# Transposing a layer norm by DMA out of DRAM in place of TensorE, from the fifth token tile on

## The chip, the core and the metric

The kernel runs on one core of a Trainium2 chip. A core has engines that run in parallel, each working through its own instructions in a fixed order: PE (matrix multiply, and transposes as a kind of matmul), DVE (vector work), ACT (activation functions, here mostly exponentials and some copies), POOL (small vector work) and SP, which in this kernel only issues DMA transfers. SBUF is the on-chip memory with 128 partitions, PSUM is where PE writes its results, and DRAM lies outside the core. An engine that reaches an instruction whose input isn't there waits, and everything behind it on that engine waits too. The metric is the device time of one execution in microseconds (us); less is better.

## What is computed

Two kinds of blocks are applied in turn, twice: attention with 32 heads of size 20, and a two-layer perceptron that mixes over the tokens. S is 2048 tokens, D is 640 features, F is 1536. All inputs are bf16.

```python
def _A_ref(x, wqkv, wo):                       # attention block
    qkv = (x @ wqkv).reshape(B, S, 3, H, Dh)   # (then transposed to 3, B, H, S, Dh)
    scores = jnp.einsum("bhqd,bhkd->bhqk", q, k) * (Dh ** -0.5)
    p = _softmax(scores, axis=-1)
    o = jnp.einsum("bhqk,bhkd->bhqd", p, v)
    return o.transpose(0, 2, 1, 3).reshape(B, S, D) @ wo

def _B_ref(x, w1, b1, w2, b2):                 # token-mixing perceptron
    h = _layernorm(x, axis=-1)
    u = _gelu(jnp.einsum("bsd,sf->bdf", h, w1) + b1)
    y = jnp.einsum("bdf,fs->bds", u, w2) + b2
    return y.transpose(0, 2, 1)

x = x + _A_ref(_layernorm(x), wqkv, wo)
x = x + _B_ref(_layernorm(x), w1, b1, w2, b2)
# ... and the same two lines once more
```

"Layer 0" and "layer 1" below are the first and the second pair of these lines.

## The kernel before

**Tiles.** The 2048 tokens are 16 token tiles of 128. For Q, K and V the layer norm of x is needed with the features on the partitions, so each normalized token tile (128 tokens x 640 features) is transposed in five squares of 128 x 128 into the buffer `hT`, which lies in the region `hh` and is 5 x 2048 columns wide. Attention works in units of a query block of 512 tokens, a group of four heads (there are eight groups) and a key tile of 128 tokens; each unit has four chunks, one for each head. A chunk is a score matmul (line 700, on PE), an exponential, and a value matmul (line 927). The exponential of most chunks is one ACT instruction (line 887, two or three chunks each); for the rest DVE builds it from one step on each chunk (line 840) and five on each unit (line 860).

**How a token tile gets to be transposed.** `token_tile` (line 521) makes the statistics on DVE (lines 343 to 346), the reciprocal root on POOL (354 and 356), applies both on DVE (line 530) into one of three bf16 buffers `hbf`, held by the ring `rHB`, and calls `transposes` (line 537). That one queues five PE transposes against an identity (line 541) into a PSUM bank and one copy of 128 x 640 from there into `hT` on ACT or DVE (line 547; in the profile the helper's lines 461 and 463). The buffer goes back to the ring when PE has read it. `got_hT` then releases the V projection of this tile, and, when four tiles are there, the K projections of these four for the first four groups (and for the first four tiles Q too). So a K projection waits for four tiles at a time; K1, K2 and K3 are those of tiles 4 to 7, 8 to 11 and 12 to 15.

**Where the tiles come from.** In layer 0 they are loaded from the input at the start (`front`, line 1556, `load_x0`), into eight buffers that come free when the tile has been applied. In layer 1 each is the result of the perceptron's second matmul in layer 0 (`add_mm2`, line 1327), which runs tile by tile while layer 1's attention has already begun on the first four tiles. Each such tile is also stored (`x2d`).

**What sets the order.** The program plans itself when it is built: every engine has a queue of jobs with a due rank and a planned duration, `run_until` picks the job that can begin first by the planner's clock, and the order so found is fixed in the program. Work that fills PE between the units of attention, such as projections and transposes, goes through `add_fill`; during attention two PSUM banks (5 and 7) serve these fills and the scores for DVE. All DMAs of `dma` (line 270) are issued by SP in one order; the planner takes 420 ns for an issue, and at most eight are open at a time. A DMA with `needs` is planned only after another one is planned to have landed. On the chip the order stays as planned, whatever the true durations are.

Of the kernel before, what the change touches and what calls it, by code (L numbers as in the profile page):

```python
# [11 lines left out]
BF16 = mybir.dt.bfloat16  # L12
# [8 lines left out]
D = 640  # L21
H = 32
DH = 20
NG = 8
NDT = D // 128
# [29 lines left out]
FILL_FIRST = False  # L55
MM1_U = ((280, 384), (408, 470))
VLATE = 1.0
PAD_V = 450.0
N_WARM0 = 10
STEPS0 = ((0, 4), (4, 16))  # L60
# [8 lines left out]
LAT_V = 120.0  # L69
EXP_CH = 453.0  # L70
D_SLACK = 0.0
WIN_S = (160.0, 160.0)
FILL_OVER = 0.0
M_F = 0.0
SD_WAIT = 500.0
# [7 lines left out]
DMA_RATE = 400.0  # L83
# [43 lines left out]
def kernel(  # L127
# [12 lines left out]
    nc = tc.nc  # L140
    S = A_x.shape[1]
    F = B_w1.shape[1]
    assert A_x.shape[2] == D
    NT = S // 128
    NKT = NT
# [11 lines left out]
    dpool = ctx.enter_context(tc.tile_pool(name="dpool", bufs=1, space=DRAM))  # L157
    mem = ctx.enter_context(tc.tile_pool(name="mem", bufs=1))
    psp = ctx.enter_context(tc.tile_pool(name="psp", bufs=1, space=PSUM))
    x1d = [dpool.tile([S, D], F32, name=f"x1d{i}") for i in range(2)]  # L160
    x2d = dpool.tile([S, D], F32, name="x2d")
    uacca = [dpool.tile([F, D], F32, name=f"uacca{i}") for i in range(2)]
    uacc = [dpool.tile([F, D], F32, name=f"uacc{i}") for i in range(2)]

# [102 lines left out]
    landed = {}  # L267
    dma_last = deque(maxlen=8)

    def dma(out_, in_, nbytes, ready=0.0, then=None, rate=DMA_RATE, key=None, needs=None, prio=1):  # L270

        def when():
            return max([ready] + ([dma_last[0]] if len(dma_last) == 8 else []) + ([landed[needs]] if needs else []))

        def f(start):
            nc.sync.dma_start(out=out_, in_=in_)
            dma_clk[0] = max(dma_clk[0], start + DMA_LAT) + nbytes / rate
            land = dma_clk[0] + 600.0
            dma_last.append(land)
            if key is not None:  # L280
                landed[key] = land
            if then:
                then(land)
        push("SP", prio, when, 420.0, f, ok=(lambda: needs in landed) if needs else None)
# [230 lines left out]
    def make_producer(L):  # L515
        def load_wv():
            L.wv = sb("wv", [128, NDT, D], BF16)
            dma(L.wv[:], A_wqkv[:, 2 * D:3 * D].rearrange("(dt p) n -> p dt n", p=128), 128 * NDT * D * 2,
                then=lambda t: setattr(L, "wv_ready", t))

        def token_tile(tt, src, ready, release=None):

            def got_stats(mv, r):
                scale_job(0, r, mv, lambda rt, nmr, r2: apply_(mv, rt, r2), False)

            def apply_(mv, rt, r):
                def f(start):
                    sl = rHB.take()
                    h_bf = sb("hbf", [128, D], BF16, sl)
                    nc.vector.tensor_scalar(out=h_bf[:], in0=src, scalar1=mv[:, 0:1], scalar2=rt[:, 0:1],  # L530
                                            op0=ALU.subtract, op1=ALU.mult)
                    if release:
                        release(start + 450)
                    transposes(h_bf, sl, start + 450 + LAT_V)
                push("DVE", 1 if tt < 4 else 2, r, 450, f, ok=lambda: len(rHB) > 0)

            def transposes(h_bf, sl, r):
                mms = []
                for dt_ in range(NDT):
                    def mm(t, dt_=dt_):  # L540
                        pe(nc.tensor.transpose(t[:, dt_, :], h_bf[:, dt_ * 128:(dt_ + 1) * 128], ident[:]))
                    mms.append(mm)

                def evac(eng, t, s, e):
                    if L.hT is None:
                        L.hT = sb("hh", [128, NDT, S], BF16)
                    copy(eng, L.hT[:, :, tt * 128:(tt + 1) * 128], t[:])
                    got_hT(tt, e)
                add_fill(mms, 64.0, evac, 420.0, ready=r, pr=L.need[("T", tt // 4)] - 0.5, urgent=lambda: L.urgent(("T", tt // 4)), acost=720.0, eprio=0.5, bf16=[128, NDT, 128],
                         after=lambda t: rHB.give(sl, t + LAT_PE))  # L550
            prio = 1 if tt < 4 else 2
            stats_job(prio, ready, src, got_stats)

        def got_hT(tt, ready):
            tb = tt // 4
            L.h_left[tb] -= 1
            if L.h_left[tb] == 0:
                for g in range(L.nearly):
                    if tb == 0:
                        add_proj("Q", g, 0, ready)  # L560
                    add_proj("K", g, tb, ready)
            add_v(tt, ready)

        def add_v(tt, ready):
            for half, (c0, c1) in enumerate(COLS):
                key = ("V", tt, half)

                lo, hi = L.last_step, NKT * L.nearly
                pr = L.need[key] + 0.5 if half == 0 else lo + (hi - lo) * VLATE * (tt + 1) / NT
                mms = []  # L570
                for dt_ in range(NDT):
                    def mm(t, dt_=dt_, c0=c0, c1=c1):
                        mmul(t[:, 0:c1 - c0], lhsT=L.hT[:, dt_, tt * 128:(tt + 1) * 128],
                                            rhs=L.wv[:, dt_, c0:c1], start=(dt_ == 0), stop=(dt_ == NDT - 1))
                    mms.append(mm)

                def evac(eng, t, s, e, c0=c0, c1=c1, half=half):
                    copy(eng, Vv[:, tt, c0 // DH:c1 // DH, 0:DH], t[:, 0:c1 - c0].rearrange("p (h i) -> p h i", i=DH))
                    L.v_ready[(tt, half)] = e
                    L.v_left[half] -= 1  # L580
                    if half == 0 and L.v_left[0] == 0:
                        producer_done()
                add_fill(mms, 136.0, evac, 400.0, ready=lambda: max(ready, L.wv_ready), pr=pr,
                         urgent=lambda pr=pr: pr <= L.now_unit() + URG, acost=460.0, ok=lambda: L.wv_ready is not None)

        def add_proj(what, g, b, ready):
            w = wk_pad if what == "K" else wq_pad
            tb = b
            key = (what, g, b)
            mms = []  # L590
            for dt_ in range(NDT):
                def mm(t, dt_=dt_):
                    mmul(t[:, :], lhsT=w[:, dt_, g, :], rhs=L.hT[:, dt_, tb * 512:(tb + 1) * 512],
                                        start=(dt_ == 0), stop=(dt_ == NDT - 1))
                mms.append(mm)
            box = {}

            def on_start(s):
                if what == "Q":
                    box["slot"] = rQ.take()  # L600

            def evac(eng, t, s, e):
                if what == "Q":
                    L.qslot[(b, g)] = box["slot"]
                    L.QT[(b, g)] = sb("QT", [128, 512], BF16, box["slot"])
                    dst = L.QT[(b, g)][:]
                else:
                    if g not in L.KT:
                        L.KT[g] = sb("KT", [128, S], BF16, g)
                    dst = L.KT[g][:, tb * 512:(tb + 1) * 512]  # L610
                copy(eng, dst, t[:, :])
                L.qk_ready[key] = e
                L.kq_left -= 1
                if L.all_kq and L.kq_left == 0:
                    L.on_hT_dead()
            L.kq_left += 1
            pr = L.need[key]
            if what == "Q" and b == LASTQB:

                pr = min(pr, L.need[("Q", 0, b)] + g)  # L620
            add_fill(mms, PE_MM, evac, 600.0, ready=ready, pr=pr, ok=lambda: w_left[what] == 0 and (what == "K" or len(rQ) > 0),
                     urgent=lambda: pr <= L.now_unit() + URG, acost=620.0, on_start=on_start, what=what)

        def producer_done():
            L.prod_done = True
            for g in range(L.nearly, NG):
                for tb in range(NQB):
                    add_proj("K", g, tb, 0.0)
                add_proj("Q", g, 0, 0.0)
            for qb in range(1, NQB):  # L630
                for g in range(NG):
                    add_proj("Q", g, qb, 0.0)
            L.all_kq = True

        L.load_wv, L.token_tile = load_wv, token_tile

    def make_attention(L):
# [4 lines left out]
        a_ptr = [0]  # L642
# [459 lines left out]
        L.opt_J, L.do_J, L.opt_T, L.do_T, L.d_take, L.opt_exp, L.do_exp = opt_J, do_J, opt_T, do_T, d_take, opt_exp, do_exp  # L1102
        L.urgent = urgent
        L.next_slot = lambda: nS[0] % 2
        L.now_unit = lambda: a_ptr[0]
        L.x1last = {}

# [293 lines left out]
    def pe_choose():  # L1401
# [5 lines left out]
        opts = []  # L1407
        s_at[0] = 1e18
        if a is not None and not a.done:
            sa = a.opt_SA()  # L1410
            if sa is not None:
                s_at[0] = st_(sa, "row")
                opts.append((s_at[0], 0, WIN_S[a.next_slot()], a.do_SA))
            sd = a.opt_SD()
            if sd is not None:
                opts.append((st_(sd, "row"), 0.9, 120, a.do_SD))
# [240 lines left out]
```

## Time and profile before

| | |
|---|---|
| runs | 1769.47, 1761.27 and 1764.65 us; median 1764.65 |
| profiled execution | 1763.39 us; span of the trace 1761.6 us; mean PE clock 0.992 |
| PE transposes (line 541) | 160, of 219 ns each |
| copies of transposed tiles | 19 on ACT (692 ns), 13 on DVE (480 ns) |
| DMA | 98.10 MB, 17.6% of the 16 DMA engines' time on SP's queue |

A line of the profile has the engine, the line of the kernel, the operation, output <- inputs, the shape and the number of instructions. In a timeline the first two numbers are start and length in us, several equal instructions may be merged (x12), and the bracket at the end gives the idle time before it and the instruction that ended it. A group that names several numbers in ns gives least, median and greatest. Matmuls overlap, so that busy time of PE is not the time at its peak.

### The profile page before, as it was taken

The page shows a single profiled execution, that of the slowest core. Times are in us where ns is not written, and L with a number is a line of the kernel's source. Part 1 is how long each engine was busy: PE and PEld are TensorE (multiplying, and loading weights), DVE is VectorE, ACT ScalarE, POOL GpSimd, SP SyncE. Part 2 cuts the span into 40 slices and gives each one's busy share as a digit, 9 for nine tenths or more (in the row PEclk, how much of TensorE's full clock was granted, in tenths as well). Part 3 has the DMA queues.
Part 4 walks back from the last instruction along what each step waited for, and adds up shares of the span by engine and source line. Part 5 has one row for each costly group of instructions (what it writes and reads, how often), then busy time and mean ns, then how long its engine had stood idle before and what let it go on. Part 6 is the DMA issues. An engine that isn't in the chain of part 4 may idle for free.

```text
span 1761.6 us, 50941 instructions
## 1 busy us (share of the span) xinstructions
PE 1673.1 (95%) x22105; PEld 644.4 (37%) x22105; DVE 1531.1 (87%) x2715; ACT 1589.0 (90%) x1441; POOL 181.1 (10%) x297
## 2 busy tenths in 40 slices
PE   8999999999999999998999999999999999999989
PEld 3433233222333233334545432332333333333356
DVE  6788999999989999998444699999998999989973
ACT  7799999999999999997598799999999999999940
POOL 3100012000200020002100000210012000200010
PEclk8999999999999999999999999999999999999999
DMA  3200001000222015520422000100012210365133
GB/s 117 28 2 2 2 13 35 1 2 1 62 71 63 17 40 183 164 62 21 141 71 81 32 2 2 39 24 1 1 31 70 69 59 1 122 181 174 46 96 97
DMA packets 103298, 98.10 MB, mean 56 GB/s; under 512 B 45600, under 2 KB 79520, under 8 KB 103072
## 3 DMA queue, kind: packets, MB, share of 16 engines
q1 hardware_dynamic: 99456, 94.82, 17.6%
q8 instruction: 173, 2.83, 0.7%
q0 software_dynamic: 3616, 0.01, 0.3%
q14 instruction: 53, 0.43, 0.1%
HBM read 63.35 MB, written 31.46 MB: 54 GB/s over the span
## 4 chain that ended last, share of the span: by engine, by line
PE 45%; DVE 41%; ACT 7%; issue 4%; DMA 2%; POOL 1%; SPq 0%; DVEq 0%; POOLq 0%; ACTq 0%
DVE JT L860 17%; PE pst L456 15%; DVE JT L840 14%; PE pst L700 12%; PE pst L927 12%; ACT P L887 6%; PE pst L453 5%; DVE T_85 L976 2%; DVE attnT L1003 1%; DMA W<-in_B_w_dram 1%; DVE QT L463 1%; DVE x1last L1088 1%; DVE bnst L343 1%; DVE bnst L344 1%; DVE rden L988 1%
## 5 line engine op out<-in xcount | busy, mean ns | idle before, releaser
L887 ACT ACTIVATE P<-pst 128x1024 bf16<-128x1024 f32 (+1 forms) x1321 | 1512.5, 1273 | 42.8 <-PE pst L700 26.3
L860 DVE TENSOR_SCALAR JT<-JT 128x2048 uint16<-128x2048 uint16 x995 | 669.7, 703 | 3.2
L700 PE MATMUL pst<-QT,KT 32*128 32x512 bf16 (+1 forms) x4224 | 577.0, 377 | 33.9 <-ACT P L887 20.7
L840 DVE TENSOR_SCALAR JT<-pst 128x512 uint16<-128x512 f32 x796 | 528.0, 677 | 66.9 <-PE pst L700 47.7
L927 PE MATMUL pst<-P,Vaug 128*32 128x512 bf16 (+1 forms) x3396 | 516.3, 380 | 3.1 <-DVE T_85 L976 2.2
L927 PE MATMUL pst<-JT,Vaug 128*32 128x512 bf16 (+1 forms) x4140 | 499.9, 376 | 14.7 <-DVE T_85 L976 9.1
L700 PEld LDWEIGHTS <-KT 32*128 32x128 bf16 x4224 | 155.1, 91 | 501.4 <-issue 492.5
L927 PEld LDWEIGHTS <-Vaug 128*32 128x32 bf16 x7536 | 181.9, 94 | 319.3 <-issue 284.8
L995 POOL TENSOR_TENSOR T_86<-T_85,rden 128x512 bf16<-128x512 f32 x64 | 68.2, 1065 | 1184.4 <-DVE rden L988 1144.7
L1466 PE MATMUL pst<-ident,zw 128*32 128x512 bf16 (+1 forms) x390 | 125.7, 376 | 0.0
L456 PEld LDWEIGHTS <-W 128*32 128x32 bf16 x3384 | 88.7, 96 | 63.3 <-issue 31.5
L456 PE MATMUL pst<-wo,attnT 128*32 128x320 bf16 x1984 | 105.2, 301 | 3.7 <-DVE JT L840 1.4
L456 PE MATMUL pst<-hh,wq 128*32 128x512 bf16 x1232 | 102.9, 382 | 2.3 <-DVE JT L840 1.8
L456 PE MATMUL pst<-hh,wk 128*32 128x512 bf16 x1240 | 96.9, 381 | 1.5 <-DVE hh L463 0.7
L456 PE MATMUL pst<-x1last,W 128*32 128x320 bf16 x1536 | 81.6, 301 | 0.4
L456 PEld LDWEIGHTS <-attnT 128*32 128x32 bf16 x1984 | 49.6, 95 | 48.4 <-issue 32.4
L456 PE MATMUL pst<-attnT,hh 128*32 128x320 bf16 x1196 | 58.9, 300 | 3.2 <-ACT hh L461 0.7
L456 PE MATMUL pst<-JT,W 128*32 128x320 bf16 x1080 | 52.6, 300 | 0.3 <-issue 0.3
L1003 DVE STREAM_TRANSPOSE attnT<-T_86 128x512 bf16<-128x512 bf16 (+1 forms) x66 | 44.9, 682 | 2.1 <-POOL T_86 L995 2.0
L1466 PEld LDWEIGHTS <-zw 128*32 128x32 bf16 x390 | 35.2, 96 | 31.1 <-issue 17.3
L456 PE MATMUL pst<-hh,W 128*32 128x320 bf16 x768 | 40.5, 301 | 6.0 <-DMA W<-in_B_w_dram 4.7
L456 PEld LDWEIGHTS <-wq 128*32 128x32 bf16 x1232 | 32.6, 95 | 34.4 <-issue 20.2
(94 smaller groups left out, 893.4 us busy)
## 6 DMA issues: line engine op xcount, KB each, us to landing
W<-in_B_w_dram SPq DMA_DIRECT2D x10, 768.0 KB
W<-in_B_w_dram SPq DMA_DIRECT2D x24, 256.0 KB
xs<-in_A_x_dram SPq DMA_DIRECT2D x32, 160.0 KB
x2d<-xs SPq DMA_DIRECT2D x16, 320.0 KB
xs<-x2d SPq DMA_DIRECT2D x16, 320.0 KB
x1d_69<-xs SPq DMA_DIRECT2D x12, 320.0 KB
uacca_72<-W SPq DMA_DIRECT2D x12, 320.0 KB
W<-uacca_72 SPq DMA_DIRECT2D x12, 320.0 KB
```

Source lines behind the costliest of these rows:

```text
L343: nc.vector.bn_stats(out=bst[:, 0, :], in_=src[:, 0:half])
L453: nc.tensor.matmul(out_, lhsT=lhsT, rhs=rhs, start=start, stop=stop)
L456: nc.tensor.matmul(out_[32 * c:32 * c + 32], lhsT=lhsT[:, 32 * c:32 * c + 32], rhs=rhs, start=start, stop=stop, tile_position=(0, 32 * c))
L700: pe(nc.tensor.matmul(dst, lhsT=k_, rhs=q_, start=True, stop=True, tile_position=(32 * j, 0)))
L840: nc.vector.tensor_scalar(out=c["jt"][:, j * 512:(j + 1) * 512], in0=Dt[:], scalar1=SCALE * LOG2E * 256.0, scalar2=127.0 * 256.0, op0=ALU. ...
L860: nc.vector.tensor_scalar(out=tt_[:], in0=c["jt"][:], scalar1=0.5, scalar2=TERM_C[i], op0=ALU.mult, op1=ALU.add)
L887: nc.scalar.activation(out=P[:, 0:n, :].rearrange("p a b -> p (a b)"), in_=St[:, 0:n, :].rearrange("p a b -> p (a b)"), func=ACT.Exp, scal ...
L927: pe(nc.tensor.matmul(dst, lhsT=Vaug[:, n:n + 32], rhs=ap, start=acc["cnt"][j] == 1 and not part, stop=last[j] and (half is None or part = ...
L976: nc.vector.transpose(out=T1[:], in_=src[:, 0:w])
L995: eng.tensor_tensor(out=T2[:], in0=T1v, in1=rden.unsqueeze(2).to_broadcast([128, w // 32, 32]), op=ALU.mult)
L1003: nc.vector.transpose(out=attnT[(qb, g)][:, q0:q1], in_=T2[:].rearrange("p c i -> p (c i)"))
L1466: pe(nc.tensor.matmul(dst[0:32, 0:128 * n], lhsT=zw[:, 0:32], rhs=ident[:].unsqueeze(1).to_broadcast([128, n, 128]), start=not inside, sto ...
```

## The change

For token tiles 4 to 15, in both layers, the normalized tile isn't transposed on PE. It is stored to a DRAM buffer `hd` (160 KB a tile), and after every second tile five transposing DMAs read 256 tokens x 128 features each out of `hd` and write 128 x 256 into `hT`. The store gives the `hbf` buffer back when it has landed; `got_hT` is called for both tiles when the fifth transposing DMA is planned to have landed. All of these DMAs are issued on SP, with rank 0.5, ahead of ordinary transfers (rank 1). The planner gives a transposing DMA the same 420 ns of issue and half the ordinary rate. The other edits give the score window a value for each stage (all equal to the old ones) and add a condition to the rank of the second half of V.

```diff
+T_DMA = 4
-WIN_S = (160.0, 160.0)
+WIN_S = ((160.0, 160.0), (160.0, 160.0), (160.0, 160.0))
...
+    hd = [dpool.tile([S, D], BF16, name=f"hd{i}") for i in range(2)]
...
         def f(start):
-            nc.sync.dma_start(out=out_, in_=in_)
+            if transpose:
+                nc.sync.dma_start_transpose(out_, in_)
+            else:
+                nc.sync.dma_start(out=out_, in_=in_)
...
             def transposes(h_bf, sl, r):
+                if tt >= T_DMA:
+
+                    dma(hd[L.layer][tt * 128:(tt + 1) * 128, :], h_bf[:], 128 * D * 2, r, then=lambda t: rHB.give(sl, t), key=("h", L.layer, tt),
+                        prio=0.5)
+                    if tt % 2:
+                        if L.hT is None:
+                            L.hT = sb("hh", [128, NDT, S], BF16)
+                        for dt_ in range(NDT):
+                            def got(t, dt_=dt_):
+                                if dt_ == NDT - 1:
+                                    got_hT(tt - 1, t)
+                                    got_hT(tt, t)
+                            dma(L.hT[:, dt_, (tt - 1) * 128:(tt + 1) * 128], hd[L.layer][(tt - 1) * 128:(tt + 1) * 128, dt_ * 128:(dt_ + 1) * 128],
+                                256 * 256, needs=("h", L.layer, tt), then=got, rate=DMA_RATE * 0.5, transpose=True, prio=0.5)
+                    return
...
-                pr = L.need[key] + 0.5 if half == 0 else lo + (hi - lo) * VLATE * (tt + 1) / NT
+                pr = L.need[key] + 0.5 if half == 0 or L.nearly > NG // 2 else lo + (hi - lo) * VLATE * (tt + 1) / NT
...
+        L.stage = lambda: 0 if not L.prod_done else 1 if a_ptr[0] < NG * NKT else 2
...
-                opts.append((s_at[0], 0, WIN_S[a.next_slot()], a.do_SA))
+                opts.append((s_at[0], 0, WIN_S[a.stage()][a.next_slot()], a.do_SA))
```

More of the change, by code (lines that the diff above doesn't have):

```diff
@@ L268, with dma @@
     dma_last = deque(maxlen=8)
-    def dma(out_, in_, nbytes, ready=0.0, then=None, rate=DMA_RATE, key=None, needs=None, prio=1):
+    def dma(out_, in_, nbytes, ready=0.0, then=None, rate=DMA_RATE, key=None, needs=None, prio=1, transpose=False):
         def when():
```

## The prediction, made before the changed kernel had run

> **What bounds the kernel now.** I read the page first, then the stretches by window, the timelines of PE, ACT, DVE and SP in the two places where the layer norm is transposed, and last the built order of both kernels, which shows what stands behind what on each in-order engine.
>
> ```profile
> PE 1673.1 (95%) x22105; PEld 644.4 (37%) x22105; DVE 1531.1 (87%) x2715; ACT 1589.0 (90%) x1441; POOL 181.1 (10%) x297
> ```
> Over the span these three engines share the limit. By window (length, then busy PE, PEld, DVE, ACT, POOL, then clock and DMA):
>
> ```profile
> 30.00:42.00 12.00, 11.36 (x136) 4.32 (x138) 9.39 (x21) 11.98 (x11) 2.05 (x6) 1.00 0.06 15
> 42.00:54.00 12.00, 10.44 (x169) 4.85 (x166) 8.92 (x16) 7.54 (x10) 6.79 (x3) 1.00 0.65 43
> 935.00:978.00 43.00, 41.26 (x773) 21.50 (x768) 15.88 (x32) 35.08 (x39) 3.36 (x9) 1.00 0.21 70
> ```
> At 42 to 54 no engine is full: this stage waits on a chain. At 935 to 978, the last layer-0 tiles, PE is the limit (96%).
>
> ```profile
> 43.38 3.71 ACT L887 ACTIVATE P<-pst 128x1536 bf16<-128x1536 f32 x3 [0.21 <-PE pst L700]
> 52.30 0.45 PE L541 MATMUL pst<-ident,attnT 128*128 128x128 bf16 x5
> 53.75 0.62 PE L456 MATMUL pst<-hh,wk 128*32 128x512 bf16 x8 [0.66 <-DVE hh L463]
> 55.10 13.68 ACT L887 ACTIVATE P<-pst 128x1024 bf16<-128x1024 f32 x12 [2.26 <-PE pst L927]
> 72.81 1.25 PE L456 MATMUL pst<-hh,wk 128*32 128x512 bf16 x20
> ```
> In layer 0 the exponentials stop at 47.1 and resume at 55.1 because the keys of tiles 8 to 11 wait for their transposes; those of tiles 12 to 15 are made at 72.8 (K3). I take K3 as the mark of this stage.
>
> ```profile
> 44.56 0.68 DVE L463 CAST KT<-pst 128x512 bf16<-128x512 f32 x1
> 22.32 1.11 DVE L530 TENSOR_SCALAR attnT<-xs,mv,rt 128x640 bf16<-128x640 bf16 x3
> L276 SPq DMA_DIRECT2D x2d<-xs x16: 319/423/862, 843.5 to 972.1; - x16
> L461 ACT COPY hh<-pst x19: 692/692/699, 10.3 to 975.2; 128x640 bf16<-128x640 bf16 x19
> L463 DVE COPY hh<-pst x13: 435/480/492, 12.1 to 895.1; 128x640 bf16<-128x640 bf16 x13
> ```
> The first line copies out the keys of tiles 4 to 7 for group 0 (K1), ready at 45.2; an ordinary DMA issue holds SP 0.42 us.
>
> [...] The trace has 219 ns on PE, five overlapped in 0.45 us; no run yet shows the DMA. [...] the first transpose of a group waits for the stores' semaphores. [...]
>
> **The change, part by part.**
> *Removed:* 12 tiles in each of 2 layers: 120 PE transposes, 24 x 0.45 = 10.8 us of PE, and 24 copies; the built order has 22 fewer on ACT (15.2 us) and 2 fewer on DVE. Neither is all on the path: in layer 0 the stage waits on the chain; in layer 1 PE is the limit: 12 x 0.45 = 5.4 us, with 1.6 us of short PE idles around these transposes, together 7.
>
> *Two edits of no effect:* the windows by stage hold the same 160, and the V priority needs more than four early groups, which there are not.
>
> *Added, with an unknown price:* 24 stores of 160 KB and 60 transposing DMAs, all on SP. Let t be the time for which one holds SP. Lower end 0.42, as an ordinary issue; [...]
>
> *Layer 0.* The built order of SP is: x of tile 12, stores of tiles 4 to 11, 20 transposes, store 12, x of tiles 13 to 15, stores 13 to 15, 10 transposes, the wo loads. The buffer ring for normalized tiles holds three, and each is now held until its store has landed. A 160 KB transfer lands about 2.4 us after issue begins (x of tile 0: issued at 0.74, used at 3.10). Applies of tiles 4 to 6 end at 23.4 as now; three stores land at 25.6 to 26.5, tiles 7 to 9 follow, their stores land from 28.5, and the store of tile 11 is issued by 29.9. Twenty transposes end at 29.9 + 20 x 1.31 = 56.1; x of tile 13 is issued at 56.5 and lands at 58.9. On DVE the statistics of tiles 13 to 15 stand **ahead of the copy of K1**, which is followed by V copies and exponential work. Three statistics (1.0 each) end at 61.9, two applies at 62.8, and K1's copy at 63.5, 18 us later than now. PE stops meanwhile: K1 and V of tile 4 hold the two spare banks. From K1 to K3 it is now 72.8 - 45.2 = 27.6 us; the 8.0 us pause at 47 falls away, as tiles 8 to 11 are long there, and transposes worth about 1 us more outside it: 18.6. K3 comes at 82.1, **9 us later**. Its own data is no limit: stores 13 to 15 are issued by 64, and ten transposes from about 65 land by 80.
>
> *Layer 1.* Summed in built order with the durations of the trace, PE work between the end of tile 7 and K1 is 12.9 us, tile 11 to K2 12.4, tile 15 to K3 9.3. The chain needs 2.7 (statistics, scale, apply, as 971.4 to 974.6 now), 2.4 (store), 5t and some 1.4 to land: 13.1. Waits: 0.2, 0.7 and 3.8. The x1 loads between transposes come a few us later, for which I allow 2. Sum 6.7 - 7 = about 0.
>
> The remaining stages have the same work: 796 + 995 DVE exponential steps, 4224 score matmuls and 7536 value matmuls in both built orders. So the sum is 9 us on a span of 1761.6. That execution took 1763.4, the runs 1761.3 to 1769.5, median 1764.65: forecast **1774 us** (+0.5%).
>
> **The rivals.**
> *A, cheap issue, faster.* If t is about 0.5, twenty transposes end at 40, tile 13 is there at 43, when DVE gets to it, and K1's copy comes near 47.5: K3 at about 68 to 70, 4 us early. In layer 1 the chain takes 9 us, inside the fill work: 7 us gained. 1765 - 11 = 1754. [...] The deciding point: at t = 1.08 the 20 x t gives K3 at 77.4, 4.6 us lost, and layer 1 gains about as much (7 less a wait of 2.6 at K3).
> *B, hidden.* The delay is at the front and the static order absorbs some of it, or t lies near 1: 1765, within 4. For it: ACT and DVE have idle in 60 to 100 (84% and 79% busy). Against: DVE's queue is fixed, and whatever it lost stays behind the stall.
> *C, squares in series.* t = 2.62: twenty end at 82.3, K1's copy at 89.7, the second group of transposes ends near 118, K3 at 119.5: 47 us lost. Layer 1 waits 6.7 + 7.2 + 10.3 = 24, less 7: 17. 1829. For it: two squares in each instruction. [...]
>
> **How the numbers follow.** What these runs can tell from no change is about 0.5%, 8.8 us. Forecast case 0.47, A 0.24, B 0.20, C 0.09. The forecast case spans t from 1.15 to 1.6: 1768 to 1785. About a quarter of it falls within 0.5%, and a sliver of A: faster 0.22, same 0.34, slower 0.44. The range takes most of A, down to 1752, at the low end and reaches to t near 2 at the high one, 1803. The likeliest case alone: 1768 to 1785.
>
> **What would show it.** On SP, transposes 1.3 us apart in two blocks of 20 and 10, then x of tile 13 after 50 us; on DVE, an idle of over 10 us before the statistics of tile 13, put down to that load; K1's copy after 60. In layer 1, PE idle of a few us before the K3 matmuls on a transpose. No L541 beyond the first four tiles, 40 in all. It is wrong if transposes follow each other at 0.5 us, if DVE goes on by itself at 45, or if PE waits in other stages[...].

## The result, and the profile after

| | before | after |
|---|---|---|
| median of the runs, us | 1763.94 (1761.27 to 1769.47) | 1793.91 (1791.96 to 1797.16) |
| span of the trace, us | 1761.6 | 1791.9 |
| first and last layer-mark, us | 821.6, 1705.5 | 843.4, 1736.0 |

The changed kernel is slower: ratio 1.0168, 95% interval 1.0139 to 1.0197, 30 us. The marks in the last row are the first start and the last start of the matmuls `pst<-hh,KT` (line 453 before, 458 after), the perceptron's first matmul on the last four token tiles: the first of them falls near the end of layer 0, the last near the end of layer 1. So **layer 0 lost 21.8 us and layer 1 another 8.7** (1736.0 - 843.4 = 892.6, against 883.9). In kernels below whose layer 0 transposes as before does, the first mark still moves, from 2.6 us earlier to 3.0 later; that is how far one trace can be read. Where two kernels were not timed beside each other, differences are taken between their ratios, times 1764.

The page of after has the same work in a longer span:

```profile
PE 1671.5 (93%) x21968; PEld 638.6 (36%) x21968; DVE 1530.5 (85%) x2713; ACT 1578.0 (88%) x1418; POOL 180.2 (10%) x297
```

PE's busy time has hardly fallen, 1673.1 to 1671.5, though 120 transposes are gone. The mean clock of PE fell from 0.992 to 0.980, and the column PEclk below shows where in layer 0. Windows of after over the start of layer 0 (length, busy PE, PEld, DVE, ACT, POOL, PE clock, DMA):

```profile
30.00:45.00 15.00, 13.15 (x136) 3.58 (x136) 10.17 (x19) 11.14 (x10) 0.74 (x2) 0.78 0.23 56
45.00:60.00 15.00, 0.91 (x15) 0.28 (x12) 0.00 (x0) 0.24 (x1) 0.00 (x0) 0.68 0.25 58
60.00:75.00 15.00, 10.25 (x86) 3.22 (x85) 12.91 (x21) 8.06 (x7) 9.04 (x9) 0.64 0.78 75
75.00:95.00 20.00, 19.58 (x354) 9.61 (x354) 18.12 (x31) 14.00 (x17) 0.00 (x0) 1.00 0.27 53
```

From 45 to 60 us all compute engines stand. From 60 to 75 they run again, but PE at 0.64 of its clock; before, the same stretch has 1.00. SP's timeline in after shows what they stand for (start, length, line, operation, count):

```profile
23.09 7.35 SPq L281 DMA_DIRECT2D hd_72<-attnT  x8
30.53 27.45 SPq L279 DMA_TRANSPOSE hh<-hd_72  x20
58.08 0.52 SPq L281 DMA_DIRECT2D hd_72<-attnT  x1
58.65 1.40 SPq L281 DMA_DIRECT2D xs<-in_A_x_dram  x3
65.06 5.59 SPq L281 DMA_DIRECT2D hd_72<-attnT  x3
70.75 13.97 SPq L279 DMA_TRANSPOSE hh<-hd_72  x10
```

Twenty transposing DMAs hold SP for 27.45 us, 1.37 each, and x of tiles 13 to 15 is issued behind them. The group line of the tile gives the time of one (least, median, greatest in ns):

```profile
L279 SPq DMA_TRANSPOSE hh<-hd_72 x30: 1102/1240/2294, 30.5 to 83.5; - x30
```

VectorE in after, from its last operation before the stop:

```profile
42.42 0.69 DVE L880 TENSOR_SCALAR JT<-JT 128x2048 uint16<-128x2048 uint16 x1
61.00 0.49 DVE L348 BATCH_NORM_STATS2 bnst<-xs 128x6 f32<-128x320 bf16 x1 [17.90 <-DMA xs<-in_A_x_dram]
...
62.05 0.64 DVE L978 COPY JT<-pst 128x512 f32<-128x512 f32 x1
...
65.30 0.69 DVE L468 CAST KT<-pst 128x512 bf16<-128x512 f32 x1
65.90 4.38 DVE L535 TENSOR_SCALAR attnT<-xs,mv,rt 128x640 bf16<-128x640 bf16 x1
```

It is idle for 17.90 us until x of tile 13 has landed. Two things stand behind those statistics: the copy that saves an attention accumulator (line 978), at 62.05, and K1's copy, at 65.30 (44.56 before). The apply of tile 15 then takes 4.38 us in place of 0.45. ScalarE's timeline of after:

```profile
36.09 8.54 ACT L907 ACTIVATE P<-pst 128x1536 bf16<-128x1536 f32 x7 [1.28 <-PE pst L720]
63.45 2.37 ACT L907 ACTIVATE P<-pst 128x1024 bf16<-128x1024 f32 x2 [18.21 <-PE pst L947]
```

And TensorE's:

```profile
62.74 1.04 PE L947 MATMUL pst<-P,Vaug 128*32 128x512 bf16 x8 [16.84 <-DVE JT L978]
...
91.52 0.61 PE L461 MATMUL pst<-hh,wk 128*32 128x512 bf16 x8
```

PE stopped at 45.9 because its next value matmuls had to wait for the copy of line 978, and ACT followed PE. K3 begins at 91.5: 72.8 before, 82.1 in the forecast.

A smaller stop comes first:

```profile
31.74 1.03 PE L720 MATMUL pst<-QT,KT 32*128 32x512 bf16 x5 [3.19 <-DVE KT L468]
```

That copy of keys stands behind the applies of tiles 7 to 11 on VectorE, which wait for the stores to give their buffers back (2.24, 0.98 and 1.12 us). PE's clock is 0.50 from 30 to 35. The kernel with one DMA and early clearing below has the same stop (3.09 us), and its layer 0 loses only 1.1, so this isn't the main loss.

In layer 1 the pair of tiles 6 and 7 shows the chain. SP in after:

```profile
910.22 0.43 SPq L281 DMA_DIRECT2D hd_73<-attnT  x1
910.75 0.40 SPq L281 DMA_DIRECT2D W<-in_B_w_dram  x1
...
913.74 0.34 SPq L281 DMA_DIRECT2D hd_73<-attnT  x1
918.81 6.97 SPq L279 DMA_TRANSPOSE hh<-hd_73  x5
```

From the issue of the second store to the first transposing DMA, which waits for that store, are 5.1 us. In between nothing is issued. Ahead of the store stands `W`, a load of 768 KB of the perceptron's second weights; two transfers of 320 KB between the two are left out here. PE in after, for K1:

```profile
923.94 1.04 PE L461 MATMUL pst<-hh,wk 128*32 128x512 bf16 x8 [2.01 <-DMA hh<-hd_73]
925.73 0.62 PE L461 MATMUL pst<-hh,wk 128*32 128x512 bf16 x4 [0.76 <-DMA hh<-hd_73]
927.06 0.62 PE L461 MATMUL pst<-hh,wk 128*32 128x512 bf16 x4 [0.71 <-DMA hh<-hd_73]
```

K adds up over the five feature blocks, so its matmuls follow the DMAs one by one, some 1.3 us apart, with 0.62 us of work and 0.7 of waiting. The four matmuls take 0.62 us here and 0.40 at full clock. By windows, PE in after is busy 127.7 of the 140 us from 870 to 1010, at clock 0.95; before, over the same work, which lies some 22 us earlier (848 to 988), 135.8 at 1.00. That is 8.1 us less busy and 0.05 x 127.7 = 6.4 of clock, less the 5.4 us of transposes that are no longer done: 9.1, beside 8.7 by the marks.

### The profile page after: what moved, and what is told of

It reads as the page before. It is cut to its first block, busy times and chain, and to the rows that moved or that the text cites. A ratio compares the mean times of both kernels' runs of the same rounds, so it can differ in the third digit from the quotient of the medians.

```text
span 1791.9 us, 50770 instructions
## 1 busy us (share of the span) xinstructions
PE 1671.5 (93%) x21968; PEld 638.6 (36%) x21968; DVE 1530.5 (85%) x2713; ACT 1578.0 (88%) x1418; POOL 180.2 (10%) x297
## 4 chain that ended last, share of the span: by engine, by line
DVE 44%; PE 41%; ACT 5%; issue 4%; DMA 3%; SPq 3%; POOL 1%; DVEq 0%; ACTq 0%; POOLq 0%
DVE JT L880 18%; DVE JT L860 15%; PE pst L461 13%; PE pst L720 12%; PE pst L947 12%; PE pst L458 5%; ACT P L907 5%; SPq L279 2%; DVE T_87 L996 2%; DVE attnT L1023 2%; DVE QT L468 1%; DVE x1last L1108 1%; DVE rden L1008 1%; DVE bnst L348 1%; DVE bnst L349 1%
## 5 line engine op out<-in xcount | busy, mean ns | idle before, releaser
L1487 PE MATMUL pst<-ident,zw 128*32 128x512 bf16 (+1 forms) x373 | 120.3, 375 | 0.0
L461 PE MATMUL pst<-hh,wk 128*32 128x512 bf16 x1240 | 102.1, 391 | 13.1 <-DMA hh<-hd_73 11.4
L461 PE MATMUL pst<-attnT,hh 128*32 128x320 bf16 x1196 | 64.3, 318 | 5.1 <-DVE Vaug L468 2.6
L461 PEld LDWEIGHTS <-wk 128*32 128x32 bf16 x1240 | 33.2, 97 | 48.1 <-issue 32.4
L359 POOL TENSOR_SCALAR rt<-mv 128x1 f32<-128x1 f32 x64 | 13.0, 203 | 339.2 <-DVE mv L351 338.4
L1396 DVE SCALAR_TENSOR_TENSOR xs<-pst,b_t,xs 128x320 f32<-128x320 f32 x24 | 13.1, 551 | 39.2 <-PE pst L461 34.8
```

Of the source, the lines that this page charges most:

```text
L461: nc.tensor.matmul(out_[32 * c:32 * c + 32], lhsT=lhsT[:, 32 * c:32 * c + 32], rhs=rhs, start=start, stop=stop, tile_position=(0, 32 * c))
L1487: pe(nc.tensor.matmul(dst[0:32, 0:128 * n], lhsT=zw[:, 0:32], rhs=ident[:].unsqueeze(1).to_broadcast([128, n, 128]), start=not inside, sto ...
```

## The experiments

The theory from these traces: in layer 0 twenty holds of SP delay x of tile 13 and, through VectorE's fixed order, everything; in layer 1 the chain store, landing, five holds is longer than the work that PE has meanwhile. Rivals: the holds themselves are the loss wherever they stand; the planner's wrong cost of an issue is; the DRAM trip (store and landing) is.

| run | what it is | ratio to before, 95% | layer 0, layer 1 by the marks, us |
|---|---|---|---|
| after | the change | 1.0168 [1.0139, 1.0197] | +21.8, +8.7 |
| e1_x_first | x ahead of the transposes | 1.0170 [1.0141, 1.0200] | +21.5, +3.6 |
| e6_stores_first | x and all stores ahead | 1.0103 [1.0079, 1.0128] | +10.0, +9.1 |
| e4_true_cost | planner told 1380 ns | 1.0070 [1.0043, 1.0096] | +5.1, +6.9 |
| e2_layer1_only | layer 1 alone | 1.0059 [1.0039, 1.0079] | +1.4, +8.7 |
| f2_keep_warm | e2, gaps filled on PE | 1.0035 [1.0021, 1.0048] | +2.0, +3.3 |
| c3_w2_after_store | e2, W load behind stores | 0.9966 [0.9951, 0.9981] | +1.7, -6.2 |
| e3_one_dma | one DMA per pair | 1.0018 [1.0004, 1.0032] | +9.4, -7.3 |
| e7_one_memset | e3, memset early | 0.9976 [0.9964, 0.9989] | +1.1, -5.2 |
| e5_one_layer1 | one DMA, layer 1 alone | 0.9971 [0.9960, 0.9981] | +3.0, -6.4 |
| e8_one_layer1_cost | e5, planner told 1330 ns | 0.9968 [0.9958, 0.9978] | -2.6, -5.5 |
| c2_best | e8, memset early | 0.9966 [0.9953, 0.9979] | -1.3, -3.6 |
| c1_before_memset | before, memset early | 1.0002 [0.9992, 1.0011] | +2.0, +0.5 |

### Layer 0: x of tile 13 first

```diff
                 dma(tl[:], A_x[0, tt * 128:(tt + 1) * 128, :], 128 * D * 2, t,
-                    then=lambda t: L0.token_tile(tt, tl[:], t, lambda t: rX0.give(sl, t)))
+                    then=lambda t: L0.token_tile(tt, tl[:], t, lambda t: rX0.give(sl, t)), prio=0.4)
```

> The changed kernel with one edit: the loads of x in layer 0 get rank 0.4, so that SP issues those of tiles 13 to 15 before the transposes and not behind twenty of them. Theory (order on SP): the 17.9 us idle of DVE before the statistics of tile 13 goes, K1's copy comes near 48 (65.3 in the changed kernel), and the next limit is the transposes themselves, 30 at 1.4 us: K3 near 78 in place of 93. Total about 1794 - 14 = 1780. Rival (the transposed data is late in itself, whatever stands behind it): K1's copy stays near 65, total 1790 or more.

1793.58 us, no gain: missed. VectorE's timeline in this run:

```profile
61.32 0.45 DVE L535 TENSOR_SCALAR attnT<-xs,mv,rt 128x640 bf16<-128x640 bf16 x1 [18.85 <-DMA hd<-attnT]
```

The load no longer stands behind the transposes, but the store of tile 12 does, and an apply waits for the buffer that this store frees. The same wait has only changed its name. So the wait for x of tile 13 was only the first of two behind the same block of twenty. (The traced execution of this run took 1788.4 us, 5 less than the median, so its marks understate the loss.)

### Layer 0: all stores ahead of the transposes

On top of the edit above:

```diff
-                                256 * 256, needs=("h", L.layer, tt), then=got, ...
+                                256 * 256, needs=("h", L.layer, tt if L.layer else NT - 1), then=got, ...
```

> The changed kernel, five transposing DMAs a pair, but in layer 0 nothing that DVE waits for stands behind a transpose: x loads first, and the 30 transposes wait until the store of tile 15. Theory (two costs: what stands behind the block, and the block itself): no DVE idle over 5 us on a DMA after the stores; the block of 30 x 1.38 = 41 us runs from about 42 to 84, K1 about 58, K3 about 86 (93 in the changed kernel, 73 before): 1794 - 7 = 1787. Rival (only the things behind the block cost): layer 0 as before, 1764 + 10 = 1774.

1781.65 us, between the two. SP in this run:

```profile
27.21 14.21 SPq L281 DMA_DIRECT2D hd<-attnT  x11
41.48 40.14 SPq L279 DMA_TRANSPOSE hh<-hd  x30
```

Once the stores are out, at 41.4, VectorE has no further wait on a DMA up to 60 us, and PE is busy for 13.3 of the 15 us from 45 to 60 (0.9 in after). About 12 of the 21.8 us come back, so that much belonged to what stood behind the transposes. The other 10 stay, with K3 at 82.4, and this run doesn't part them. The thirty holds take 40 us in any order; but PE also stops for 9.35 us up to 41.7, while VectorE does the statistics and applies of all tiles up to 15 in one go. The last of these applies takes 3.30 us; a slow one like it comes up below, beside a clearing on GpSimd.

### The planner told the true cost

```diff
-        push("SP", prio, when, 420.0, f, ok=(lambda: needs in landed) if needs else None)
+        push("SP", prio, when, 1380.0 if transpose else 420.0, f, ok=(lambda: needs in landed) if needs else None)
```

> The changed kernel with one number changed: the planner takes 1380 ns, as measured, for the issue of a transposing DMA (420 before). SP's order in layer 0 stays the same (the x loads of tiles 13 to 15 still behind 20 transposes), but DVE, ACT and PE are ordered for it. If the loss is mostly a plan made for the wrong duration, about half of it comes back: 1775 to 1783. If it is mostly the SP time itself, 1788 or more.

1775.06 us: 17 of the 30 us back. SP's order in layer 0 is as in after, twenty transposes from 30.4 to 57.0 and x of tile 13 behind them. What differs is the order on the other engines; ACT in this run:

```profile
44.57 13.86 ACT L907 ACTIVATE P<-pst 128x1024 bf16<-128x1024 f32 x12 [0.38 <-PE pst L947]
```

Where ACT in after is idle for 18.21 us, it works here: the planner knew that the transposes last to 57 and put attention into that time. So the wait for SP costs little by itself; most of layer 0's loss (21.8 to 5.1) came from an order made for holds of 420 ns.

### Layer 1 alone

```diff
-                if tt >= T_DMA:
+                if tt >= T_DMA and L.layer == 1:
```

> Only layer 1 transposes by DMA; layer 0 is as before the change. It splits the loss of 30 us. By marks in the two traces layer 0 loses about 20 us and layer 1 about 10: expected 1764 + 10 = 1774. If the prediction's balance for layer 1 (7 gained, 7 lost) were right and all of the loss came from layer 0: 1764.

1774.49 us, a hit: layer 1 loses the same 8.7 with layer 0 on TensorE. So layer 1's loss doesn't hang on layer 0's. (Layer 0 alone was not run.)

### One DMA in place of five

```diff
-                        for dt_ in range(NDT):
-                            def got(t, dt_=dt_):
-                                if dt_ == NDT - 1:
-                                    got_hT(tt - 1, t)
-                                    got_hT(tt, t)
-                            dma(L.hT[:, dt_, (tt - 1) * 128:(tt + 1) * 128], hd[L.layer][(tt - 1) * 128:(tt + 1) * 128, dt_ * 128:(dt_ + 1) * 128],
-                                256 * 256, ...
+                        def got(t):
+                            got_hT(tt - 1, t)
+                            got_hT(tt, t)
+                        dma(L.hT[:, :, (tt - 1) * 128:(tt + 1) * 128], hd[L.layer][(tt - 1) * 128:(tt + 1) * 128, :],
+                            256 * 256 * NDT, ...
```

> The five transposing DMAs of a pair of tiles become one, of 256 tokens x 640 features into 128 x 5 x 256: the same bytes, a fifth of the instructions. Theory (each instruction holds SP for a fixed time of about 1.3 us, whatever its size): one hold of 1.3 to 2 us for a pair, tile 13 no longer waits, no DMA wait of PE in layer 1: 1752 to 1760, faster than before the change. Rival (the hold goes with the size): 5 x 1.38 = 6.9 us for each, 1790.

1766.14 us. The part on the hold came out; the group line of this run:

```profile
L279 SPq DMA_TRANSPOSE hh<-hd x12: 1263/1333/1715, 30.2 to 976.7; - x12
```

320 KB hold SP for 1.33 us, 64 KB for 1.24. Between these two sizes the time goes with the instruction and not with its bytes or squares. Layer 1 gains 7.3, but the total missed, as layer 0 still lost 9.4. VectorE's timeline in this run, at the apply of tile 15:

```profile
46.35 4.42 DVE L535 TENSOR_SCALAR attnT<-xs,mv,rt 128x640 bf16<-128x640 bf16 x1
```

And GpSimd's, at the same time:

```profile
45.98 4.61 POOL L1619 MEMSET wo<- 128x5120 bf16 x1
```

GpSimd clears `wo_pad` over just this time. In after the two coincide as well (apply 65.90 to 70.28, clearing 65.74 to 70.10). The next two runs test that.

```diff
         nc.gpsimd.memset(Vaug[:, NKT * H * VW:], 0.0)
+        nc.gpsimd.memset(wo_pad[:].rearrange("p a b -> p (a b)"), 0.0)
...
     def late_weights():
-        nc.gpsimd.memset(wo_pad[:].rearrange("p a b -> p (a b)"), 0.0)
```

> One DMA a pair in both layers, and POOL's clearing of wo, 4.4 us, moved to the start of the kernel, where POOL waits anyway. In the changed kernel and with one DMA the DVE apply of tile 15 took 4.4 us in place of 0.45, at the time of this memset. If the memset holds the DVE instruction up: the apply takes 0.45 to 0.9 us, V copies and exponentials follow 4 us earlier, 1766 - 4 = 1762. If the time has another cause: apply still 4.4 us, 1766.

1758.57 us, more than expected: 7.4 us less than with the clearing in its old place, and layer 0 is back to +1.1. The apply now, with the clearing at 2.10 us:

```profile
46.14 1.01 DVE L535 TENSOR_SCALAR attnT<-xs,mv,rt 128x640 bf16<-128x640 bf16 x1
```

The same edit in the kernel before:

> The kernel before with the clearing of wo_pad moved to the start of GpSimd's work and nothing else. If the 7.6 us that the same move gained with one large transposing DMA per pair came only from the apply of token tile 15 that lay beside the clearing there (4.4 us instead of 0.45) and from what followed it, this kernel gains nothing, because before has the clearing at 41.7 to 46.1 us, where none of VectorE's applies lies: 1762 to 1766 us. Rival: the early clearing is worth as much in any kernel (the weights behind it on the queue come earlier, or the planner places other work): 1756 to 1758.

1763.97 us beside 1763.25: nothing. The clearing costs only where an apply meets it, and in before none does (clearing from 41.71 to 46.08, applies up to 38.41 and from 49.80). Beside the clearing an apply took 4.38 us in after and 4.42 with one DMA, apart from it 0.45 to 1.01; why it is slower there was not shown. That the move gains 7 us and not 4 lies in what follows the apply. PE with the clearing in its old place:

```profile
51.41 0.62 PE L945 MATMUL pst<-JT,Vaug 128*32 128x512 bf16 x4 [2.77 <-DVE JT L878]
```

With the early clearing the longest wait of these matmuls for VectorE's exponentials is 0.4 us. Windows of the two kernels from 50 to 65 us, the old place first:

```profile
50.00:65.00 15.00, 13.59 (x114) 4.33 (x117) 8.78 (x14) 7.58 (x7) 3.26 (x3) 0.54 0.74 68
50.00:65.00 15.00, 14.84 (x210) 5.69 (x201) 12.80 (x23) 14.68 (x14) 0.00 (x0) 1.00 0.49 79
```

PE comes back at half its clock. Its 13.59 us of matmul time at 0.54 are worth 0.46 x 13.59 = 6.3 us less than at 1.00, more than the wait itself. How the 7.4 us divide between the two was not measured.

With one DMA in layer 1 alone, then with its cost told to the planner (1330 in place of 420 ns), then with the early clearing as well:

> One transposing DMA for a pair of tiles, in layer 1 alone; layer 0 transposes on PE as before the change. By the marks of the run with one DMA in both layers, layer 0 lost 9.4 us there and layer 1 gained 7.3. If the two are independent: 1764 - 7 = 1757, faster than both kernels. If the gain of layer 1 was only work put off from layer 0: 1764.

> As the kernel with one DMA in layer 1 alone, and the planner takes the measured 1330 ns for its issue. With one transposing DMA a pair the plan is hardly wrong, so little should come of it: within 3 us of 1757. If the plan's duration is what matters even here: 4 us or more faster.

> One large transposing DMA per pair of token tiles in layer 1 alone, its true time given to the planner, TensorE's transposes in layer 0, and the early clearing of wo_pad. Theory: layer 0 has no apply beside the clearing, so it adds nothing to the 1757.3 of the same kernel without it: 1755 to 1759. Rival (the early clearing gains in any kernel): about 1750.

1758.01, 1757.26 and 1758.07 us, all as expected. They are one and the same within their intervals: six holds are too few for the planner's cost to matter, and layer 0 has no apply beside the clearing.

### Layer 1: the load ahead of the stores

```diff
-                    rate=DMA_RATE * 0.75, prio=0 if sp < 2 else 1, then=lambda t: L.w2.update({sp: (tl, sl, t)}))
+                    rate=DMA_RATE * 0.75, prio=0 if sp < 2 else 0.45 if L.nxt and sp > 3 else 1,
+                    needs=("h", 1, 2 * sp - 3) if L.nxt and sp > 3 else None, then=lambda t: L.w2.update({sp: (tl, sl, t)}))
```

> Five transposing DMAs per pair in layer 1 alone, as in the run of layer 1 alone (1774.5), but the 768 KB loads of the FFN's second weights, which stand just ahead of the stores in four of the six pairs, are issued behind the stores. If those loads hold the stores up, the time from a store's issue to the first transposing DMA falls from 4 to 5 us to 1.8 to 2.4 in these pairs, and about 3 to 4 us of layer 1's loss of 9 come back: 1770 to 1772. Rival: the stores are late for another reason, or TensorE has other work for that time: still 4 to 5 us, or a total of 1773 to 1776.

1757.43 us: right in direction, and 16 us come back where 3 to 4 were expected. SP in this run, for the pair that has 4.7 us from store to first transpose in the run of layer 1 alone:

```profile
931.39 0.34 SPq L281 DMA_DIRECT2D hd<-attnT  x1
931.82 0.39 SPq L281 DMA_DIRECT2D W<-in_B_w_dram  x1
933.33 7.58 SPq L279 DMA_TRANSPOSE hh<-hd  x5
```

Here it is 1.9 us. The four pairs with a load have 3.1, 4.0, 5.2 and 1.9 us (4.8, 6.4, 5.0 and 4.7 in the run of layer 1 alone); the load now starts right behind the store, and in three of the four the time is not below that of the two pairs without a load here (3.1 and 1.8). So only 1.7 us a pair were saved on average, and yet the whole loss of layer 1 is gone, with a gain of 6.2 in its place. The windows from 870 to 1010 say why: PE is busy 133.0 us at clock 1.00, against 126.5 at 0.93 in the run of layer 1 alone. That is 6.5 us of waiting and up to 0.07 x 126.5 = 8.9 of clock (not all of it need lie on the path). I had counted the wait alone. That the planner also ordered other work differently here was not ruled out.

### Layer 1: the clock by itself

```diff
                 def mm(t, dt_=dt_):
+                    if what == "K" and L.layer == 1 and tb > 0 and L.k_first.setdefault(tb, g) == g and dt_ > 0:
+                        for _ in range(3):
+                            nc.tensor.matmul(t[0:32, :], lhsT=zw[:, 0:32], rhs=ident[:].unsqueeze(1).to_broadcast([128, 4, 128]),
+                                             start=False, stop=False, tile_position=(0, 0))
                     mmul(t[:, :], lhsT=w[:, dt_, g, :], rhs=L.hT[:, dt_, tb * 512:(tb + 1) * 512],
```

> Five transposing DMAs per pair in layer 1 alone, as in the run of layer 1 alone (1774.5), with three matmuls of zeros, which leave the sum as it is, ahead of the second to fifth step of the first projection K of each block of 512 tokens: 36 small matmuls in all, laid into the 0.8 to 0.95 us that TensorE waits there for each next transposing DMA. No DMA, wait or order is changed otherwise. Theory: half of layer 1's loss is TensorE's clock, which in that run falls to 0.5 to 0.74 in the ten microseconds after each such stretch of short matmuls and waits (in sum some 10 us of matmul time between 870 and 1010 us): with the gaps filled the clock stays above 0.9 there and 6 to 9 us come back, 1765 to 1769, the waits for transposes staying at 13 us or so (as waits of the zeros and what follows). Rival: the clock falls in stretches where TensorE has to wait anyway, and its loss costs nothing: 1773 to 1776, whatever the clock. If the clock falls all the same, the run tells nothing of its cost.

1767.72 us. PE in the run of layer 1 alone, two of the five steps of K1 and the V matmuls behind them:

```profile
905.44 0.40 PE L461 MATMUL pst<-hh,wk 128*32 128x512 bf16 x4 [0.91 <-DMA hh<-hd]
906.79 0.40 PE L461 MATMUL pst<-hh,wk 128*32 128x512 bf16 x4 [0.95 <-DMA hh<-hd]
910.26 2.06 PE L461 MATMUL pst<-attnT,hh 128*32 128x320 bf16 x28
```

Windows around K1 in that run (the columns as above):

```profile
905.00:910.00 5.00, 2.85 (x29) 0.82 (x28) 0.58 (x2) 0.58 (x1) 0.00 (x0) 0.74 0.49 143
910.00:915.00 5.00, 5.00 (x59) 2.27 (x61) 3.16 (x7) 3.39 (x3) 0.74 (x2) 0.57 0.91 268
```

The same two windows in this run:

```profile
905.00:910.00 5.00, 4.24 (x46) 1.73 (x38) 0.63 (x2) 0.00 (x0) 0.12 (x1) 1.00 0.20 45
910.00:915.00 5.00, 4.62 (x78) 2.24 (x76) 2.83 (x7) 3.23 (x4) 0.74 (x2) 1.00 0.82 233
```

And PE's timeline of this run, two steps of K1 with the zeros (line 616) between, and the same V matmuls:

```profile
906.93 0.40 PE L461 MATMUL pst<-hh,wk 128*32 128x512 bf16 x4 [0.23 <-DMA hh<-hd]
907.14 0.81 PE L616 MATMUL pst<-ident,zw 128*32 128x512 bf16 x3
908.21 0.40 PE L461 MATMUL pst<-hh,wk 128*32 128x512 bf16 x4 [0.26 <-DMA hh<-hd]
912.20 1.14 PE L461 MATMUL pst<-attnT,hh 128*32 128x320 bf16 x28
```

K's matmuls come no sooner, 1.28 us apart as the DMAs do. But the clock stays at 1.00, and the 28 V matmuls take 1.14 us in place of 2.06. (K1 is done 2.7 us later in this run, at 911.0 against 908.3, so the windows don't hold quite the same work. From there to the same score matmuls it is 3.9 us here and 6.3 in the run of layer 1 alone.)

6 to 9 us were expected; 5.4 come back by the marks, 4.2 by the ratios and 6.8 by the medians, whose runs of before differ by 2.0. The intervals of the two ratios overlap a little, from 1.0039 to 1.0048, so the size is rough. That the low clock costs time is plain at K1, and nothing but the zeros was changed. So **some 4 to 5 of the 15 us between this layer's loss and its gain are the clock after K's stuttering**. The rest was not separated further.

## Why the prediction was right or wrong

Forecast 1774, 9 us slower; measured 1793.9, 30 slower. The sign held and the time lies in the range, but not in the likeliest case's own 1768 to 1785. That the range holds it is luck: its upper end was drawn for t near 2, and t was 1.37, for which the same sum gives about 1775. Both layers lost more than forecast: layer 0 21.8 us in place of 9, layer 1 8.7 in place of about 0.

**Right.** *t = 1.31*, which no trace had shown when the prediction took it (nor its upper end, 2.62): 1.37 and 1.40 us in SP's two blocks, 1.24 as the median of one, here of two squares, and 1.33 for ten in the run with one DMA. Rivals A (0.5) and C (2.62) fall with it. *The block on SP*: forecast 29.9 to 56.1, found 30.5 to 58.0. *VectorE's idle before the statistics of tile 13*: over 10 us, found 17.90, put down to that load. *K1's copy*: done by 63.5, found 66.0. *Transposes left on PE*: 40, as the group of line 561 has it. *K3 of layer 1*: a wait of 3.8, found 4.2 (1.74 + 0.60 + 0.92 + 0.96). *The gain of 7 in layer 1 once nothing waits*: 3.6 to 7.3 in six runs, in five of which PE was seen to wait 3.5 to 5.7 us there for transposing DMAs (12.1 in after).

**Wrong: "From K1 to K3 ... 18.6".** It was 25.5 (66.0 to 91.5), and this and K1's 2.5 make K3 9.4 us later than forecast; 3 more are lost after it. The term took what PE and ACT do behind K1 at the pace of before. Two prices were missing. PE came back at clock 0.64 from 60 to 75, so its 10.25 us of matmul time there are worth 0.36 x 10.25 = 3.7 us less. And the apply of tile 15 took 4.38 in place of 0.45, with PE idle for 2.01 us behind it. Removing the collision gave 7.4 us in the kernel with one DMA, by the estimate there more through the clock than through the wait; in after itself the two weren't separated. The cause I gave for PE's stop, that K1 and V hold the spare banks, was wrong as well: it was the accumulator's copy of line 978, which stands behind the statistics of tile 13 on VectorE. And most of the loss belongs to the order and not to the holds as such: planned with the true cost, layer 0 loses 5.1 us at nearly the same t (26.61 us for twenty).

**Wrong: "the chain needs 2.7 ..., 2.4 (store), 5t and some 1.4 to land: 13.1".** At K1 of layer 1 it was 4.3 (end of the tile's matmul, some 909.5, to the start of the store after the apply) + 5.1 + 7.0 + about 1.3 to land = 17.7. The largest miss is the store: 4.1 to 5.1 us in the four pairs with the 768 KB load ahead of it; in the two without, 1.84 and 1.83, less than the 2.4. So K1 and K2 waited 3.5 and 3.7 us, not 0.2 and 0.7. I had read the 2.4 off the first load of the kernel, which has nothing ahead of it. The three waits are 11.4 us in place of 4.7. Less the 7 gained that leaves 4.4 of the 8.7, and the 4 to 5 of the clock, as the run with the zeros shows them, about make up the rest.

**Wrong by omission: the clock.** Nothing in the sum priced what a wait does to PE afterwards. In the 16.84 us stop of layer 0 the clock fell to 0.53 (50 to 55 us) and 0.50 (55 to 65). Short waits were followed by a low clock too. At K1 of the run of layer 1 alone no wait was over 0.95 us; PE was busy for 5.8 of the 10 us from 900 to 910, and 0.57 followed from 910 to 915. And in the run with one DMA a stop of 2.77 us was followed by 12 us in which four value matmuls took 0.62 to 0.67 us in place of 0.40 (clock 0.54 from 50 to 65), though PE was never idle in them by the profile. A wait of 2.4 us for a transposing DMA in layer 1 of the run with one DMA there alone was followed by no fall: 1.00 from 870 to 1010. So in these runs the longest gap alone did not tell what the clock would do, and what followed a stop could cost more than the stop (by the estimate above 6.3 us after 2.77).

**Rival B, hidden**, was wrong for this order and right in principle: with the true cost told to the planner, most of layer 0's loss is hidden.

**The best version.** The kernels with one DMA in layer 1 alone, with and without the further edits, five DMAs in layer 1 with the load behind the stores, and one DMA in both layers with the early clearing all stand at 0.9966 to 0.9976. Each interval excludes 1, and they overlap. 4 to 6 us are to be had from this change; rival A, with a cheap issue, had hoped for 11. (Its K3 at 68 to 70 doesn't follow from the 18.6, which gives 47.5 + 18.6 = 66.1.) Which of them is best can't be told. Issuing the transposing DMAs from another engine than SP was not tried.

## What to carry to other kernels

Price a transposing DMA by the instruction, not by the byte (here 1.2 to 1.4 us of its queue for 64 KB as for 320), so make few and large ones, keep loads and buffer-freeing stores off the queue behind them (VectorE waited 17.90 and 18.85 us for such a load and such a store here), and tell the planner that price. When a change adds waits to TensorE, allow in the sum for the half clock that can follow them (here up to 12 us of it after one stop), also where the waits are short but many (0.57 after five of 0.76 to 0.95 us). A chain through DRAM is timed in the place where it runs: from the store to what waits for it took 1.8 us at the least here, and 4.1 to 6.4 behind a load of 768 KB.

## What was not expected of the hardware

- A transposing DMA holds its queue for 1.24 us with 64 KB and 1.33 us with 320 KB (medians, in after and in the run with one DMA), against 0.42 for an ordinary issue (the median of the `x2d` stores in before).
- Matmuls in steps of 0.40 us with waits of 0.76 to 0.95 between, over 6 us, were followed by a clock of 0.57 (the run of layer 1 alone, 910 to 915); with 0.81 us of zero matmuls in each of the four gaps between the steps it stayed at 1.00 (905 to 915).
- A stop of 2.77 us on TensorE was followed by 12 us in which four value matmuls took 0.62 to 0.67 us in place of 0.40, though it was busy throughout by the profile (the run with one DMA, clock 0.54 from 50 to 65).
- An apply of 128 x 640 in bf16 on VectorE, 0.45 us alone, took 4.38 us in after and 4.42 in the run with one DMA beside GpSimd's clearing of 128 x 5120; in both it ended 0.2 us after the clearing. The same apply took 4.46 us with the true cost told and 3.30 with the stores first.
- A store of 160 KB was followed by what waited for it after 1.8 to 2.2 us with no load ahead of it, and after 4.1 to 6.4 us behind a load of 768 KB (in after and in the run of layer 1 alone).
